# Signs and bucket pattern of an LSH attention over 128 rows, and a list schedule with other durations

## The chip, the cores and the metric

The kernel runs on one core of a Trainium2 chip. The metric is the device time of one execution in microseconds; the median of several executions is compared.

## What is computed

The reference is an attention in which a query sees only the keys of its own hash bucket, and two gated feed-forward layers after it.

```python
q_bits = (np.einsum('bhsd,dk->bhsk', q, proj) > 0)      # 6 bits; k the same
q_bucket = np.sum(q_bits * powers, axis=-1)             # a number from 0 to 63
mask = q_bucket[:, :, :, None] == k_bucket[:, :, None, :]
scores = np.where(mask, scale * q @ k.T, -1e9)          # then softmax, then @ v
x = ((x @ w1) * (x @ w2)) @ w3 @ w_out                  # 1536 tokens, 512 -> 1024 -> 512
out = (sigmoid(x @ w_gate) * (x @ w_val)) @ w_out2      # 512 -> 1536 -> 512
```

There are 2 batches of 8 heads, 768 positions and a head size of 64. The weights of the feed-forward layers come as 64-bit floats and are decoded to 32 bits on the chip.

## The kernel before, in words

**Attention.** The 16 heads are taken in order, each in 6 tiles of 128 queries; there are 96 such steps. A step multiplies scores for 128 queries and 768 keys (`emit_qk`, lines 465 and 468, two halves of 384 columns each), takes their maximum on VectorE (line 474), the exponential on ScalarE (line 484), turns the result by TensorE transposes (line 517), splits it into a rounded and a rest part (lines 520 and 522), and multiplies by the values (line 535). A float32 product is made of three matmuls of type float32r, rounded by rounded, rounded by rest, rest by rounded.

**The bucket mask.** `prep` (line 394) prepares a head while the one before it is computed. POOL scales and splits q and k (lines 404 to 406), and SyncE copies halves between partitions (lines 409 to 419). For each half of 384 positions `hashes` (line 383) makes the mask rows. Three matmuls (line 388) project q and k onto the 6 hash directions, with weights `pq` of 64 columns of which two groups of 6 are not zero; so the sums `ps[0:64]` have 64 rows. ScalarE takes their signs into `sg`, 64 rows (line 390). A fourth matmul (line 391) multiplies the signs by the pattern `pat`, 64 rows by 128 columns: row groups of signs against all 64 buckets, for q and for k. VectorE compares the sums with a threshold (line 413; for the first head line 451). The first head is prepared in `first_head` (line 424), the others in `prep`. The constants `pq`, `pat`, `zb` and the integer tiles `bits` are made once, in lines 800 to 824.

**Filler work.** Between the attention steps TensorE also multiplies w3 by w_out (line 590, `gen_fill`, with splits in lines 577 to 585) and does the first feed-forward layer for the first 512 tokens (`gen_first`, line 618, with splits of its input in lines 632 and 633). Each of the 76 weight pieces of 512 KB goes through a load (line 321) and `decode` (line 326): two ScalarE activations (337, 338), two POOL operations (339, 340) and two VectorE operations (341, 346). All other feed-forward work is in `moe` (line 710), behind the attention.

**The order.** Every step is emitted with a priority. `order_engines` (line 46) then plays a list schedule over all instructions emitted up to the end of `gen_first`: each engine takes the ready instruction with the lowest priority number, `cost` (line 75) says how long it holds the engine, `step` (line 92) how long its result takes to reach another engine, and lines 218 to 220 when a load has landed. The resulting order of each engine (TensorE, ScalarE, VectorE, POOL and SyncE's queue of DMAs) is then fixed by dependencies (line 227). The instructions of `moe` are emitted behind this and stand outside the list schedule.

Of the kernel before, what the change touches and what calls it, by code (L numbers as in the profile page):

```python
# [10 lines left out]
F32 = mybir.dt.float32  # L11
F32R = mybir.dt.float32r
U32 = mybir.dt.uint32
I32 = mybir.dt.int32
# [3 lines left out]
AF = mybir.ActivationFunctionType  # L18
# [10 lines left out]
class Tiles:  # L29
# [3 lines left out]
    rings = {}  # L33
# [12 lines left out]
def order_engines(tc):  # L46
# [8 lines left out]
    rings = Tiles.rings  # L55
    N = len(ins)

    def count(x):
        n = 1
        for _, c in list(x.ap)[1:]:  # L60
            n *= c
        return n
# [12 lines left out]
    def cost(k):  # L75
        i, e, op = ins[k], eng[k], type(ins[k]).__name__
        rd = [x for x in i.ins if hasattr(x, "ap")]
        n = max([count(i.outs[0])] + [count(x) for x in rd[:1]])
        if e == "PE":
            passes = 1 if "float32r" in str(rd[0].dtype) else 2 if n == 128 else 4  # L80
            return n / 2.4 * passes + 2.5
        if e == "Activation":
            return 971 if n == 768 else 50 + n * 0.836
        if e == "Pool":
            return 60 + n * 2.3
        if e == "DVE":
            if op in ("InstTensorTensor", "InstTensorReduce") or (op == "InstTensorScalarPtr" and len(rd) > 1 and count(rd[1]) > 8):
                return 69 + n * 1.04
            return 585 if op == "InstTensorScalarPtr" and n == 384 else 69 + n * 0.52
        return 600  # L90

    step = {("Activation", "DVE"): 145, ("Activation", "PE"): 200, ("Activation", "Pool"): 170, ("DVE", "Activation"): 132,
# [53 lines left out]
    def blocked(k):  # L146
        for t in opens.get(k, ()):
            g = rings[t][0]
            if slots[g] <= 0 or queue[g][taken[g]] != t:
                return g  # L150
            if g[0] == "mw" and pools.get("wtmp"):
                return "wtmp"
        return None
# [4 lines left out]
    dma = 0.0  # L158

    def wake(g):  # L160
        for k in waiting.pop(g, ()):
            heapq.heappush(ready[eng[k]], (ins[k].bass_priority, k))

    def post(t, what, x):
        heapq.heappush(events, (t, next(tick), what, x))
# [4 lines left out]
    while events:  # L170
        now = events[0][0]
        while events and events[0][0] <= now:
            _, _, what, x = heapq.heappop(events)
            if what == "ready":
                heapq.heappush(ready[eng[x]], (ins[x].bass_priority, x))
            elif what == "slot":
                g = rings[x][0]
                slots[g] += 1
                pools[g[0]] -= 1
                wake(g)  # L180
                if not pools[g[0]]:
                    wake(g[0])
            elif what == "end":
                for u in ends[x]:
                    left[u] -= 1
                    at[u] = max(at[u], now + step.get((eng[x], eng[u]), 60))
                    if not left[u]:
                        post(at[u], "ready", u)
                for t in held.get(x, ()):
                    todo[t] -= 1  # L190
                    if not todo[t]:
                        post(now + 200, "slot", t)
        again = True
        while again:
            again = False
            for e in ranks:
                while free[e] <= now and ready[e]:
                    _, k = heapq.heappop(ready[e])
                    g = blocked(k)
                    if g is not None:  # L200
                        waiting.setdefault(g, []).append(k)
                        continue
                    for t in opens.get(k, ()):
                        g = rings[t][0]
                        slots[g] -= 1
                        taken[g] += 1
                        if slots[g] > 0 and waiting.get(g):
                            wake(g)
                            again = True
                    order[e].append(k)  # L210
                    for u in begins[k]:
                        left[u] -= 1
                        at[u] = max(at[u], now)
                        if not left[u]:
                            post(at[u], "ready", u)
                    free[e] = done = now + cost(k)
                    if e == "SP":
                        n = count(ins[k].outs[0]) * list(ins[k].outs[0].ap)[0][1] * mybir.dt.size(ins[k].outs[0].dtype)
                        dma = max(now + 1080, dma) + n / 360
                        done = dma + 900  # L220
                    post(done, "end", k)
                    post(free[e], "free", k)
# [8 lines left out]
def lsh_attention_moe_moe2_kernel(  # L231
# [20 lines left out]
    B, H, S, D = v.shape  # L252
    P = 128
    NB = proj.shape[1]
    NT = S // P
    HS = S // 2
# [13 lines left out]
    act = nc.scalar  # L270
    dve = nc.vector
    pool = nc.gpsimd
    pe = nc.tensor
# [8 lines left out]
    cst = Tiles(ctx.enter_context(tc.tile_pool(name="cst", bufs=1, side="left")), "cst", 1)  # L282
# [3 lines left out]
    psT = Tiles(ctx.enter_context(tc.tile_pool(name="psT", bufs=4, space=bass.MemoryType.PSUM)), "psT", 4)  # L286

    idf = cst.tile([P, P], F32, name="idf")
    pq_raw = cst.tile([P, NB], F32, name="pq_raw")
    pq = [cst.tile([P, D], F32R, name=f"pq{i}") for i in range(2)]  # L290
    thr = cst.tile([P, 2], F32, name="thr")
    scl = cst.tile([P, 1], F32, name="scl")
    zb = cst.tile([D, 1], F32, name="zb")
    pat = cst.tile([D, P], F32R, name="pat")
    bits = [cst.tile([D, P], I32, name=f"bits{i}") for i in range(2)]

    xall = big.tile([P, KC, NTOK], F32, name="xall")
    xraw = [xall[:, :, i * CH:(i + 1) * CH] for i in range(NSW)]
# [4 lines left out]
    psS = Tiles(att_ctx.enter_context(tc.tile_pool(name="psS", bufs=1, space=bass.MemoryType.PSUM)), "psS", 1)  # L303
    scs = [psS.tile([P, 2, 512], F32, name=f"s{i}") for i in range(2)]
    ap_ = Tiles(att_ctx.enter_context(tc.tile_pool(name="att", bufs=2, side="right")), "att", 2)
# [77 lines left out]
    def hashes(m, half):  # L383

        hs = slice(half * HS, (half + 1) * HS)
        ps = psT.tile([P, 512], F32, tag="t", name="gps")
        for n, (w, x) in enumerate(((0, "aq"), (0, "bq"), (1, "aq"))):
            pe.matmul(ps[0:D, :HS], lhsT=pq[w], rhs=m[x][:, hs], start=n == 0, stop=n == 2)  # L388
        sg = ap_.tile([D, HS], F32R, tag="sg", name="sg")
        act.activation(out=sg, in_=ps[0:D, :HS], func=AF.Sign, scale=2.0 ** 64, bias=zb)  # L390
        pe.matmul(ps[:, :HS], lhsT=pat, rhs=sg, start=True, stop=True)  # L391
        return ps

# [30 lines left out]
    def first_head():  # L424

        alloc_mats(0)
        m = mats[0]
        t = [ap_.tile([P, S], F32, tag="qk", name=f"qk0{i}") for i in range(2)]
        for r in (slice(0, D), slice(D, P)):
            sync.dma_start(out=pq_raw[r], in_=proj)  # L430
        for half in range(2):
            hs = slice(half * HS, (half + 1) * HS)
            sync.dma_start(out=t[0][:, hs], in_=qk[0][:, hs])
        for r, o in ((slice(0, D), slice(D, P)), (slice(D, P), slice(0, D))):
            sync.dma_start(out=t[1][r], in_=qk[0][o])
        load_v(0)
        yield
        for half in range(2):
            hs = slice(half * HS, (half + 1) * HS)
            act.activation(out=m["aq"][:, hs], in_=t[0][:, hs], func=AF.Copy, scale=scl[:, 0:1])  # L440
            dve.scalar_tensor_tensor(out=m["bq"][:, hs], in0=t[0][:, hs], scalar=scl[:, 0:1], in1=f(m["aq"][:, hs]),
                                     op0=ALU.mult, op1=ALU.subtract)
        load_qk(1)
        for d in ("bk", "ak"):
            pool.tensor_copy(m[d][0:D], t[1][0:D])
        act_copy(m["bk"][D:P], f(m["bq"][D:P]))
        pss = [hashes(m, half) for half in range(2)]
        act.activation(out=m["bq"][D:P], in_=t[1][D:P], func=AF.Copy, scale=SCALE)
        for d, r in (("ak", slice(0, D)), ("aq", slice(D, P))):
            for half in range(2):  # L450
                dve.tensor_scalar(out=m[d][D:P, half * HS:(half + 1) * HS], in0=pss[half][r, :HS], scalar1=thr[r, 0:1], scalar2=thr[r, 1:2],
                                  op0=ALU.is_gt, op1=ALU.mult)
        load_qk(2)
        yield
# [345 lines left out]
    start = first_head()  # L800
    next(start)
    make_identity(nc, idf)
    o = D // 2
    pool.iota(bits[0], pattern=[[0, 2], [1, D]], base=0, channel_multiplier=0)
    for r in range(0, D, o):
        pool.iota(bits[1][r:r + o], pattern=[[0, P]], base=0, channel_multiplier=1)
# [85 lines left out]
    for _ in first:  # L892
        pass
    order_engines(tc)
    prio(0, 200000)
    att_ctx.close()
# [44 lines left out]
```

## Time and profile before

| | us |
|---|---|
| median of 3 runs | 832.86 (831.72 to 833.24) |
| the profiled execution | 831.98 |
| its span, first to last instruction | 830.2 |
| TensorE busy in the span | 801.8 |
| ScalarE, VectorE, POOL busy | 513.3, 458.0, 429.5 |
| mean granted TensorE clock | 0.992 |

PE is TensorE's matmuls, PEld its loads of weights, DVE is VectorE, ACT ScalarE, SP SyncE. A row of the trace names line, engine, operation, the tiles written and read, and shapes as partitions x elements; for a matmul, 64*128 stands for weights of 64 rows and 128 columns. Matmuls are pipelined, and their ends are modelled: the distance from the start of one to the start of the next says more than the length of a record. The profiled execution took 1.8 us more than its span, and 0.9 us less than the median of the runs.

### The profile page before, as it was taken

The numbers are of one execution on the slowest core, as the hardware profiler recorded it, in microseconds if no ns is written. First come the engines' busy times: TensorE is split into PE (matmuls) and PEld (weight loads), VectorE is DVE, ScalarE is ACT, GpSimd is POOL, SyncE is SP. The second block draws the span as 40 slices with busy tenths as digits, with TensorE's granted clock in tenths as the row PEclk, the third lists the DMA queues.
The fourth block names the chain that finished last, engine by engine and source line by source line (L and its number), as shares of the span: only waits on it lengthen the run. The fifth ranks groups of instructions, "written<-read, shape, count | busy, mean of one in ns | idle before, by whom it ended". The sixth has DMA issues, their size and how long they took to land.

```text
span 830.2 us, 11487 instructions
## 1 busy us (share of the span) xinstructions
PE 801.8 (97%) x4016; PEld 657.1 (79%) x4016; DVE 458.0 (55%) x696; ACT 513.3 (62%) x944; POOL 429.5 (52%) x457
## 2 busy tenths in 40 slices
PE   5899899999999999999999999999999999999998
PEld 3577688888787888887888888888888888888886
DVE  5536787777788878977354535564522222222222
ACT  5788778787788888876455655766534333343332
POOL 5567656665466555559355556677633333333330
PEclk9999899999999999999999999999999999999999
DMA  8744547454455644131022122344001000010001
GB/s 259 199 153 129 171 125 188 130 156 112 121 147 145 147 102 128 61 137 51 1 74 79 52 77 76 103 152 135 17 1 51 1 1 1 0 52 1 0 1 51
DMA packets 28585, 74.46 MB, mean 90 GB/s; under 512 B 6128, under 2 KB 8432, under 8 KB 28528
## 3 DMA queue, kind: packets, MB, share of 16 engines
q1 hardware_dynamic: 28528, 73.73, 29.9%
q8 instruction: 32, 0.52, 0.3%
q14 instruction: 25, 0.20, 0.1%
HBM read 52.83 MB, written 3.19 MB: 67 GB/s over the span
## 4 chain that ended last, share of the span: by engine, by line
PE 86%; DVE 8%; ACT 3%; issue 1%; POOL 1%; DMA 0%; SPq 0%; DVEq 0%; POOLq 0%; ACTq 0%
PE m L695 18%; PE pa L695 17%; PE pb L695 17%; PE av L535 8%; PE tp L517 6%; PE wacc L590 5%; PE p L695 4%; PE s L465 3%; PE s L468 3%; DVE sm L474 2%; PE y L695 2%; PE gps L388 2%; DVE pt L522 2%; DVE da L341 1%; PE gps L391 1%
## 5 line engine op out<-in xcount | busy, mean ns | idle before, releaser
L735 DVE TENSOR_TENSOR pb<-pb,a 128x512 f32<-128x512 f32 x52 | 36.3, 699 | 179.0 <-PE pb L695 175.6
L474 DVE TENSOR_REDUCE sm<-s 128x1 f32<-128x768 f32 x96 | 91.0, 949 | 32.2 <-PE s L468 25.2
L689 POOL TENSOR_TENSOR wal<-xall,wah 128x512 fp32r<-128x512 f32 x36 | 46.9, 1304 | 107.2 <-ACT wah L277 107.2
L517 PE MATMUL tp<-idf,e 128*128 128x128 f32 x576 | 99.8, 278 | 1.0 <-DVE pt L522 1.0
L695 PE MATMUL pa<-x,wah 128*128 128x512 f32 x320 | 99.2, 390 | 0.0
L695 PE MATMUL pb<-x,wbh 128*128 128x512 f32 x320 | 98.6, 389 | 0.0
L520 ACT ACTIVATE pt<-tp 128x512 fp32r<-128x512 f32 (+1 forms) x144 | 82.8, 597 | 23.7 <-PE tp L517 22.6
L484 ACT ACTIVATE e<-s,sm 128x768 f32<-128x768 f32 x96 | 86.6, 902 | 13.8 <-DVE sm L474 12.4
L339 POOL TENSOR_SCALAR dr<-st 128x512 bf16<-128x512 f32 x76 | 71.0, 943 | 46.4 <-issue 25.7
L522 DVE TENSOR_TENSOR pt<-tp,pt 128x512 fp32r<-128x512 f32 x126 | 83.4, 683 | 18.1 <-ACT pt L520 17.7
L535 PE MATMUL av<-pt,spv 128*128 128x256 f32 (+1 forms) x576 | 86.0, 299 | 1.3 <-DVE pt L522 1.2
L517 PEld LDWEIGHTS tp<-idf,e 128*128 128x128 f32 x576 | 72.4, 143 | 12.5 <-issue 2.4
L535 PEld LDWEIGHTS av<-pt,spv 128*128 128x128 f32 (+1 forms) x576 | 73.7, 184 | 10.7 <-DVE pt L522 2.8
L590 PE MATMUL wacc<-wo,t 128*128 128x512 f32 x192 | 70.6, 434 | 6.3 <-ACT wo L277 2.8
L695 PEld LDWEIGHTS pa<-x,wah 128*128 128x128 f32 x320 | 60.1, 188 | 13.2
L695 PEld LDWEIGHTS pb<-x,wbh 128*128 128x128 f32 x320 | 60.1, 188 | 12.6
L465 PE MATMUL s<-bk,bq 128*128 128x384 f32 x192 | 61.8, 375 | 6.2 <-ACT e L484 5.7
L340 POOL TENSOR_SCALAR da<-da 128x512 f32<-128x512 f32 x76 | 48.3, 640 | 36.6 <-ACT da L337 32.5
L695 PE MATMUL pa<-x,wal 128*128 128x512 f32 x160 | 62.4, 391 | 0.9 <-POOL wal L689 0.9
L695 PE MATMUL pb<-x,wbl 128*128 128x512 f32 x160 | 62.5, 390 | 0.0
L468 PE MATMUL s<-ak,aq 128*128 128x384 f32 x192 | 60.2, 369 | 0.0
L338 ACT ACTIVATE dr<-st 128x512 int16<-128x512 uint32 x76 | 59.9, 788 | 0.0
(143 smaller groups left out, 1810.2 us busy)
## 6 DMA issues: line engine op xcount, KB each, us to landing
st<-in_moe_w_dram SPq DMA_DIRECT2D x32, 512.0 KB, 4.3
st<-in_moe_w_out_dram SPq DMA_DIRECT2D x20, 512.0 KB, 4.3
st<-in_moe_w_gate_dram SPq DMA_DIRECT2D x12, 512.0 KB, 3.2
st<-in_moe_w_val_dram SPq DMA_DIRECT2D x12, 512.0 KB, 3.2
qk<-in_qk_dram SPq DMA_DIRECT2D x15, 384.0 KB, 4.2
rr<-row SPq DMA_DIRECT2D x16, 192.0 KB, 3.5
out_dram<-o SPq DMA_DIRECT2D x12, 256.0 KB, 2.0
ak<-aq SPq DMA_DIRECT2D x15, 192.0 KB, 2.6
```

The costliest lines, as they stand in the source:

```text
L338: act.activation(out=r.bitcast(I16)[:, 0::2], in_=lw, func=AF.Copy, scale=2.0 ** -29)
L339: pool.tensor_scalar(out=r.bitcast(BF16)[:, 1::2], in0=f(hw), scalar1=0.0, scalar2=1.0, op0=ALU.mult, op1=ALU.mult)
L465: pe.matmul(s[:, half, :HS], lhsT=m["bq"][:, qs], rhs=m["bk"][:, ks], start=True, stop=False)
L468: pe.matmul(s[:, half, :HS], lhsT=m["aq"][:, qs], rhs=m["ak"][:, ks], start=False, stop=True)
L474: dve.tensor_reduce(out=b, in_=s[:, :, :HS], op=ALU.max, axis=AX.XY, negate=True)
L484: act.activation(out=e.rearrange("p (a c) -> p a c", a=2), in_=s[:, :, :HS], func=AF.Exp, bias=sm, scale=1.0, accum_out=su_t[h][:, t:t + 1],)
L517: pe.transpose(ps[:, i * P:(i + 1) * P], e_t[g - g % 2 + a][:, c * P:(c + 1) * P], idf)
L520: act.activation(out=dh, in_=src, func=AF.Copy)
L522: dve.tensor_tensor(out=d, in0=src, in1=f(dh), op=ALU.subtract)
L535: pe.matmul(acc[:w.shape[1], :2 * P].rearrange("p (a t) -> p a t", a=2), lhsT=w, rhs=r[:, :, c], start=(c == 0 and i == 0), stop=(c == NT ...
L590: pe.matmul(acc, lhsT=t3[x][:, j], rhs=wo[y][:, j], start=(j == 0 and n == 0), stop=(j == NF1 - 1 and n == 2))
L695: mm = pe.matmul(ps, lhsT=lhs[x], rhs=rhs[y], start=start and n == 0, stop=stop and n == 2)
```

## The change

The hash weights `pq` become 128 columns wide (the added columns are zero), so the sums fill 128 rows; the signs `sg`, their bias `zb` and the pattern `pat` get 128 rows too, of which the added rows of the pattern are zero. The integer tiles `bits` move from constants of their own into the ring of the mask tile `ft`. In the list schedule the durations of `cost` and the landing of a load are given other numbers, with a distinction between operands in PSUM and others.

```diff
@@ cost
+        banks = [x for x in rd + [i.outs[0]] if (region(x) or ("",))[0] in rings and rings[region(x)[0]][0][0] in ("psT", "psS")]
         if e == "PE":
             passes = 1 if "float32r" in str(rd[0].dtype) else 2 if n == 128 else 4
-            return n / 2.4 * passes + 2.5
+            return n / 2.4 * passes + (16 if passes == 1 else -12 if passes == 2 else 4)
         if e == "Activation":
-            return 971 if n == 768 else 50 + n * 0.836
+            return 971 if n == 768 and banks else 50 + n * (0.836 if banks else 1.0)
         if e == "Pool":
-            return 60 + n * 2.3
+            if op == "InstTensorTensor":
+                return 40 + n * 2.4 if n < 768 else 2200
+            return 100 + n * 1.15
         if e == "DVE":
+            if op == "InstCustomDveAnt":
+                return 720
             if op in ("InstTensorTensor", "InstTensorReduce") or (op == "InstTensorScalarPtr" and len(rd) > 1 and count(rd[1]) > 8):
-                return 69 + n * 1.04
-            return 585 if op == "InstTensorScalarPtr" and n == 384 else 69 + n * 0.52
+                return 69 + n * (1.04 if banks else 1.4)
+            return 585 if op == "InstTensorScalarPtr" and n == 384 else 69 + n * 0.6
@@ order_engines
-                        dma = max(now + 1080, dma) + n / 360
+                        dma = max(now + 1900, dma) + n / 300
                         done = dma + 900
@@ constants
-    pq = [cst.tile([P, D], F32R, name=f"pq{i}") for i in range(2)]
+    pq = [cst.tile([P, P], F32R, name=f"pq{i}") for i in range(2)]
-    zb = cst.tile([D, 1], F32, name="zb")
-    pat = cst.tile([D, P], F32R, name="pat")
-    bits = [cst.tile([D, P], I32, name=f"bits{i}") for i in range(2)]
+    zb = cst.tile([P, 1], F32, name="zb")
+    pat = cst.tile([P, P], F32R, name="pat")
@@ hashes
-            pe.matmul(ps[0:D, :HS], lhsT=pq[w], rhs=m[x][:, hs], start=n == 0, stop=n == 2)
-        sg = ap_.tile([D, HS], F32R, tag="sg", name="sg")
-        act.activation(out=sg, in_=ps[0:D, :HS], func=AF.Sign, scale=2.0 ** 64, bias=zb)
+            pe.matmul(ps[:, :HS], lhsT=pq[w], rhs=m[x][:, hs], start=n == 0, stop=n == 2)
+        sg = ap_.tile([P, HS], F32R, tag="sg", name="sg")
+        act.activation(out=sg, in_=ps[:, :HS], func=AF.Sign, scale=2.0 ** 64, bias=zb)
@@ setup
     make_identity(nc, idf)
+    bits = ap_.tile([P, S], F32R, tag="ft", name="bits", bufs=1).bitcast(I32)
+    bits = [bits[0:D, i * P:(i + 1) * P] for i in range(2)]
```

## Rows read from the trace of the kernel before

**Rows 1.** The page: TensorE's busy time; the core's span and clock.

```profile
PE 801.8 (97%) x4016; PEld 657.1 (79%) x4016; DVE 458.0 (55%) x696; ACT 513.3 (62%) x944; POOL 429.5 (52%) x457
...
core 0: 830.2 us, clock 0.992
```

**Rows 2.** Busy time by stage: stage, length, engines (instructions), clock, DMA share, GB/s.

```profile
0.00:20.00 20.00, 10.07 (x28) 6.29 (x29) 11.18 (x30) 11.62 (x19) 11.22 (x22) 0.96 0.81 261
20.00:40.00 20.00, 16.75 (x82) 11.71 (x82) 12.04 (x18) 14.76 (x29) 11.06 (x15) 0.93 0.75 203
...
80.00:100.00 20.00, 16.33 (x87) 13.46 (x88) 15.92 (x23) 15.04 (x30) 12.71 (x17) 0.83 0.54 162
...
220.00:240.00 20.00, 17.95 (x111) 14.74 (x111) 19.23 (x30) 17.34 (x36) 11.30 (x14) 1.00 0.47 134
...
376.00:830.00 454.00, 450.34 (x1954) 366.65 (x1954) 174.49 (x260) 215.61 (x364) 203.08 (x180) 1.00 0.13 45
...
100.00:376.00 276.00, 268.88 (x1660) 230.50 (x1658) 224.02 (x339) 223.14 (x440) 163.35 (x194) 1.00 0.48 131
```

**Rows 3.** The list of TensorE's waits: us in total, times, longest.

```profile
PE gps L388 <- ACT aq L440: 6.7, 1, 6.7
PE s L465 <- ACT e L484: 5.7, 6, 1.4
```

**Rows 4.** The timeline of TensorE from 300.7 to 302.6 us: start, length, instruction.

```profile
300.68 0.34 PE L468 MATMUL s<-ak,aq 128*128 128x384 f32 x1
300.86 0.34 PE L388 MATMUL gps<-aq,pq 128*64 128x384 f32 x1
301.04 0.39 PE L695 MATMUL p<-xl,wh 128*128 128x512 f32 x1
301.36 0.44 PE L391 MATMUL gps<-sg,pat 64*128 64x384 f32 x1
301.73 0.50 PE L695 MATMUL p<-xh,wl 128*128 128x512 f32 x1
302.07 0.39 PE L695 MATMUL p<-xh,wh 128*128 128x512 f32 x1
302.30 0.33 PE L388 MATMUL gps<-bq,pq 128*64 128x384 f32 x1
```

**Rows 5.** Pattern matmuls, from 100 to 376 us (ns: least/median/most) and in all.

```profile
L391 PE MATMUL gps<-sg,pat x22: 435/439/442, 103.7 to 322.4; 64*128 64x384 f32 x22
...
L391 PE MATMUL gps<-sg,pat 64*128 64x384 f32 x32 | 14.6, 461 | 1.2 <-ACT sg L390 1.2
```

**Rows 6.** The timeline of TensorE: the first scores.

```profile
11.29 1.62 PE L465 MATMUL s<-bk,bq 128*128 128x384 f32 x4 [0.27 <-ACT bq L448]
```

**Rows 7.** Groups of weight loads: count, busy us, mean ns, idle before.

```profile
L465 PEld LDWEIGHTS s<-bk,bq 128*128 128x128 f32 x192 | 35.2, 194 | 15.6 <-ACT e L484 10.5 <-issue 1.6 <-ACT da L337 0.3
...
L388 PEld LDWEIGHTS gps<-aq,pq 128*64 128x64 f32 x64 | 9.0, 140 | 10.2 <-ACT aq L440 7.0 <-POOL bq L406 0.9 <-issue 0.6
```

**Rows 8.** Groups of ScalarE's instructions: count, busy us, mean ns, idle before.

```profile
L520 ACT ACTIVATE pt<-tp 128x512 fp32r<-128x512 f32 x126 | 72.5, 598 | 20.9 <-PE tp L517 19.7
...
L390 ACT ACTIVATE sg<-gps,zb 64x384 fp32r<-64x384 f32 x32 | 17.8, 572 | 6.1 <-PE gps L388 5.7
```

**Rows 9.** Groups of VectorE's instructions: the memsets of the hash weights.

```profile
L813 DVE MEMSET pq<- 128x64 f32 x2 | 0.2, 112 | 0.1
```

**Rows 10.** Groups on POOL and VectorE, and loads (us to landing), whose planned durations change.

```profile
L339 POOL TENSOR_SCALAR dr<-st 128x512 bf16<-128x512 f32 x76 | 71.0, 943 | 46.4 <-issue 25.7 <-DVE w1r L346 10.1 <-DVE wc L346 5.6
L340 POOL TENSOR_SCALAR da<-da 128x512 f32<-128x512 f32 x76 | 48.3, 640 | 36.6 <-ACT da L337 32.5
...
L633 DVE TENSOR_TENSOR xl<-xall,xh 128x512 fp32r<-128x512 f32 x4 | 4.2, 1066 | 0.0
...
st<-in_moe_w_dram SPq DMA_DIRECT2D x32, 512.0 KB, 4.3
```

**Rows 11.** The timeline of TensorE in the stretch from 80 to 100 us.

```profile
87.36 0.62 PE L465 MATMUL s<-bk,bq 128*128 128x384 f32 x2 [1.32 <-ACT e L484]
```

## The prediction

> **What bounds the kernel now.** I read the busy times first. TensorE is busy for 801.8 of 830.2 us at a mean granted clock of 0.992 [rows 1], so what it does not do, and what it does slowly, is nearly the whole question. Then the busy times by stage. From 376 us on there is no hole but the last store: 450.34 busy of 454.00, and nothing that the diff touches runs there, so I take it as fixed. Everything that can move lies ahead of 376 us. From 100 to 376 us TensorE is busy for 268.88 of 276.00 us, against 224.02 for VectorE and 223.14 for ScalarE [rows 2]: TensorE is the bound there, with some 19% of room on the next two engines. The holes are in four short stretches: 9.93 us in 0:20, 3.25 in 20:40, 3.67 in 80:100 (which also has a granted clock of 0.83) and 2.05 in 220:240, where VectorE is busy for 19.23 of 20.00 us. The list of waits says what ends them: the first hash matmul waits 6.7 us for the first rounded input, and later the scores wait 5.7 us in six pieces for a softmax activation [rows 3].
>
> A busy engine can still be slow, and the busy share does not show that. So I read the matmuls one by one around a sign pattern (line 391) by their starts, since the ends are modelled [rows 4]. Of 384 columns, a score matmul (128 rows, 128 columns of weights) starts 0.18 us before the next one, and so does a hash matmul (128 rows, 64 columns). Of 512 columns, a matmul in plain sequence takes 302.07 to 302.30, 0.23. The pattern matmul has the same 384 columns but weights of 64 rows. The matmul ahead of it takes 301.04 to 301.36, 0.32 in place of 0.23; it takes 301.36 to 301.73, 0.37 in place of 0.18; the one behind it takes 301.73 to 302.07, 0.34 in place of 0.23. Together 0.09 + 0.19 + 0.11 = 0.39 us of TensorE's time that buys nothing. The group is uniform: the 22 pattern matmuls between 100 and 376 us last 435 to 442 ns, and there are 32 in all [rows 5], one for each half of each of 16 heads.
>
> **The change, part by part.** 1. *Pattern over 128 rows.* The weights and the signs fill all rows, as in every matmul around them. I take the 0.39 us as the price of changing from 128 rows to 64 and back, since the hash matmuls, which differ from their neighbours in columns only, show nothing of it. For 22 in the bound stretch: 22 x 0.39 = 8.6 us. I count nine tenths, 7.7, since that stretch is busy to 97% (268.88 of 276.00) and a little of what is freed will meet waits. Of the other ten, two stand at the start, where the scores start at 11.29 us when ScalarE's copy of line 448 is done [rows 6]: nothing gained. Eight lie between 20 and 82 us: 8 x 0.39 = 3.1, among the holes of 20:40 and 80:100; I count half, 1.6. Sum 9.3 us. Bounds: 0, if all of it turns into waits, and 8.6 + 3.1 = 11.7.
>
> 2. *Hash weights of 128 columns.* 96 matmuls of line 388 get weights twice as wide. A load of 64 columns takes 140 ns, one of 128 columns 194 [rows 7]: 96 x 0.054 = 5.2 us if the loads were exposed, nothing if they hide behind the running matmul. I take nothing: the score matmul with its 128 columns has the same 0.18 us from start to start as the hash matmul with 64. The matmul ahead of it covers the load (0.18 us against 0.194 and overlapping); without that cover it is the 5.2.
>
> 3. *Sign activation on 128 partitions.* 32 activations of 64x384 take 572 ns; the copies of 128x512 out of the same kind of tile take 598 [rows 8], so twice the partitions cost between 0 and 32 x 0.026 = 0.8 us of ScalarE, which has room. I take nothing, as a row of 384 elements stays one of 384.
>
> 4. *Setup.* Wider memsets and the bit tiles in the ring of the mask tile run while TensorE waits its first 6.7 us [rows 3]. The next user of that ring is the second head's mask, which comes behind the first head's scores at 11.29 us [rows 6]. Nothing; without the cover, the two memsets of 112 ns [rows 9] once more, 0.2 us.
>
> 5. *The list schedule.* No work is added, but every engine's order up to the end of attention and of the first token chunk can change, with SyncE's queue of loads and POOL's among them. A load out of turn holds back all that stand behind it on SyncE; a decode out of turn holds POOL's splits, and through them the matmuls that read them. What the plan believed and what the trace has [rows 10]: POOL's two decode steps were planned at 60 + 512 x 2.3 = 1238 ns each and take 943 and 640; the new 100 + 512 x 1.15 = 689 is nearer in sum (1378 against 1583, before 2476). VectorE's split of line 633 was planned at 601, takes 1066, is now 786. A 512 KB load was planned to land after 1080 + 1456 + 900 = 3.4 us, takes 4.3, is now 4.5. For TensorE, 384 columns go from 162.5 to 176, the 0.18 of the trace. So the plan comes nearer nearly everywhere, yet a list schedule answers to a small change with another order, and another order has other holes. Bounds: at best it clears the holes after the start, 3.25 + 3.67 + 2.05, and the clock lost in 80:100, 0.17 x 20 = 3.4, together 12.4 us. At worst it digs the same again, 12.4. I take a gain of 2.0, the row it is nearest to: the hole of 220:240, where line 633 holds VectorE's queue, is the one whose cause the new durations speak of most directly.
>
> The sum: the profiled execution took 831.98 us. 831.98 - 9.3 - 2.0 = 820.7. The median of the runs shown is 832.86, 0.9 above it; so 821.5 us for the median.
>
> **The rivals.** A. *The freed time turns into waits.* TensorE gets to each wait sooner, and VectorE and ScalarE, each busy for over 80% of 100:376, come last more often; 220:240 shows how that looks. For it: scores already wait for the softmax. Against it: 97% busy with only 7.1 us of holes in 276. Half of 8.6 stays, nothing of the first 100 us and nothing of the plan: 832.86 - 4.3 = 828.6 us.
>
> B. *The plan starves TensorE (slower).* Place: the fill work of the first 100 us, where matmuls of line 590 wait for a decoded and split weight. That is how 80:100 looks now: a hole of 1.32 us [rows 11] and others, 3.67 in all, and then matmuls at the lower of the two clock levels (1.2 in place of 2.4 GHz) for part of the stretch, 3.4 us. One such stall costs 7.1 us. It decides from the second one on, as one does not use up the 9.3: 832.86 - 9.3 + 14.2 = 837.8 us. For it: POOL's plan falls by 1.1 us a decode to below what is measured, so splits may be ordered to be ready sooner than they are. Against it: the loads are planned later, not earlier.
>
> C. *The plan clears that stall.* With 7.1 us of 80:100 and the 2.0 taken: 832.86 - 9.3 - 9.1 = 814.5 us. For it: later landings in the plan are just what a stall on decoded weights asks for. Against it: some hole has always been left somewhere.
>
> D. *The pattern stays dear and the hashes get dearer.* If a load of weights went beside a running matmul only where their rows differ, 128 rows after 128 rows would save nothing at the pattern, and the wider hash loads would show: 832.86 + 5.2 = 838.1 us. Against it: the score matmuls load 194 ns of 128-row weights each [rows 7] and still start 0.18 us apart [rows 4]. The Trainium skill, page "TensorE: Matmul & The Clock Gate", section "The mechanism", states this rule: loads overlap with matmuls in flight only when the row group differs. By that rule the change would lose; the trace's start to start disagrees with it, so the case gets little.
>
> **How the numbers follow.** Forecast 0.60, A 0.20, C 0.11, B 0.06, D 0.03. Predicted: the forecast's 821.5. The range runs from C's 814 to just past A's 829; B and D, and the far sides of A and C, are left out, under 2 in 10. The unknown of the schedule, not the pattern, sets its width. A change within 0.2% (1.7 us) is about what measurement cannot tell from none. Faster by more: the forecast and C, and most of A, 0.87. Within: the rest of A, 0.04. Slower: B and D, 0.09.
>
> **What would show it.** Right: in the new trace line 391 lasts about as long as line 388 (some 340 ns), starts 0.18 us ahead of the next matmul, and its neighbours are back to 0.23 for 512 columns; line 388 still starts 0.18 apart; the end of the attention comes some 11 us sooner; and the stretch behind it keeps its length to a microsecond. Wrong: line 391 still at 0.37 (D); TensorE's holes ahead of the end of attention growing by over 4 us, on waits for VectorE or ScalarE (A), or on line 590 with a granted clock under 0.9 beside it (B). The schedule is right if the holes of 220:240 and 80:100 shrink or go and none of their size comes elsewhere.

## The result and the profile after

The changed kernel takes 814.43 us (median of 4 runs, 814.15 to 815.14), the kernel before 833.05 in the runs beside it: a ratio of 0.9778, 95% interval 0.9761 to 0.9795, so 18.5 us less. Its profiled execution took 815.14 us.

The page of the changed kernel, as [rows 1]:

```profile
PE 790.9 (97%) x4016; PEld 659.0 (81%) x4016; DVE 459.3 (56%) x696; ACT 512.7 (63%) x944; POOL 432.7 (53%) x457
...
core 0: 813.4 us, clock 0.998
```

TensorE's matmuls are as many and its busy time is 10.9 us shorter; the span is 16.8 shorter. So a part of the gain is busy time that went and a part is holes that went, and the mean clock is higher too. The busy times by stage, as [rows 2] (the end of the attention lies some 17 us sooner, so the last two stages are cut at 360):

```profile
0.00:20.00 20.00, 10.10 (x24) 6.74 (x24) 12.78 (x32) 11.06 (x19) 10.71 (x21) 1.00 0.77 265
20.00:40.00 20.00, 17.89 (x92) 13.98 (x93) 10.41 (x16) 16.20 (x32) 15.09 (x21) 0.91 0.73 202
...
80.00:100.00 20.00, 18.37 (x119) 15.91 (x119) 19.94 (x31) 18.03 (x36) 15.95 (x22) 1.00 0.82 218
...
200.00:220.00 20.00, 18.56 (x120) 16.15 (x120) 16.15 (x25) 16.30 (x34) 10.02 (x14) 1.00 0.46 126
220.00:240.00 20.00, 19.44 (x125) 17.04 (x123) 18.57 (x29) 17.94 (x36) 13.49 (x16) 1.00 0.51 142
...
100.00:360.00 260.00, 255.40 (x1609) 225.63 (x1608) 213.15 (x326) 214.92 (x425) 156.07 (x181) 1.00 0.50 131
360.00:813.00 453.00, 449.69 (x1953) 366.06 (x1951) 173.89 (x259) 215.67 (x364) 202.35 (x179) 1.00 0.13 45
```

A stage's hole is its length less TensorE's busy time. The hole of 80:100 falls from 3.67 to 1.63 us, and the granted clock there goes from 0.83 to 1.00, so no part of that stretch runs at the lower level any more. It does 119 matmuls where there were 87. That of 20:40 falls from 3.25 to 2.11, with the clock still at 0.91. The hole of 220:240 falls from 2.05 to 0.56, but most of it has only moved: the stage ahead of it, 200:220, had 0.38 in the kernel before.

```profile
200.00:220.00 20.00, 19.62 (x118) 16.18 (x117) 12.41 (x19) 13.27 (x26) 10.01 (x12) 1.00 0.37 101
```

It has 1.44 now, so the two together fall from 2.43 to 2.00. From 100 us to the end of the attention the holes fall from 7.12 us (in 276) to 4.60 (in 260). The stretch behind the attention keeps its length. The matmuls of the second layer's half (tile m), first the kernel before, then the changed one; the last two times of a row are its first and last start:

```profile
L695 PE MATMUL m<-wth,gl x144: 395/396/397, 539.3 to 826.1; 128*128 128x512 f32 x144
L695 PE MATMUL m<-gh,wth x64: 392/397/400, 417.0 to 532.5; 128*128 128x512 f32 x64
```

```profile
L699 PE MATMUL m<-wth,gl x144: 395/396/397, 522.5 to 809.3; 128*128 128x512 f32 x144
L699 PE MATMUL m<-gh,wth x64: 392/397/400, 400.1 to 515.7; 128*128 128x512 f32 x64
```

From the first to the last it is 409.1 us before and 409.2 after: all 16.9 us were won ahead of it. Now the pattern matmul (line 395 in the changed kernel), in TensorE's timeline of two stretches, as [rows 4]:

```profile
286.12 0.40 PE L699 MATMUL p<-xh,wh 128*128 128x512 f32 x1
286.36 0.34 PE L395 MATMUL gps<-sg,pat 128*128 128x384 f32 x1
286.54 0.34 PE L392 MATMUL gps<-bq,pq 128*128 128x384 f32 x1
...
287.52 0.33 PE L469 MATMUL s<-bk,bq 128*128 128x384 f32 x1
287.72 0.44 PE L395 MATMUL gps<-sg,pat 128*128 128x384 f32 x1
288.00 0.34 PE L469 MATMUL s<-bk,bq 128*128 128x384 f32 x1
288.18 0.39 PE L699 MATMUL p<-xh,wh 128*128 128x512 f32 x1
```

At 286.36 nothing is left of the 0.39 us: 0.24 ahead, 0.18 for itself, 0.17 behind. At 287.72 it takes 0.28, with 0.20 ahead and 0.18 behind. This second form is common here: between 100 and 360 us the 20 records last from 333 to 446 ns, and 11 of them 440 or more. The loads of the weights show the difference, first in the kernel before with the signs that it reads, then the two of the changed kernel:

```profile
300.47 0.58 ACT L390 ACTIVATE sg<-gps,zb 64x384 fp32r<-64x384 f32 x1 [1.66 <-PE gps L388]
...
301.36 0.18 PEld L391 LDWEIGHTS gps<-sg,pat 64*128 64x128 f32 x1 [0.30 <-ACT sg L390]
```

```profile
286.20 0.19 PEld L395 LDWEIGHTS gps<-sg,pat 128*128 128x128 f32 x1
...
287.72 0.19 PEld L395 LDWEIGHTS gps<-sg,pat 128*128 128x128 f32 x1 [0.24 <-ACT sg L394]
```

Before, the load of 64 rows starts only with its own matmul, at 301.36, though the signs, which its wait names, were done at 301.05. With 128 rows it starts at 286.20, 0.16 us ahead of its matmul, and hides behind the matmul in front. At 287.72 it again starts together with its matmul, but here because the signs are only just there: the waits of this tile name ScalarE's signs as what these loads waited for (2.3 us in 9 waits between 100 and 360 us). Such a late load shows by 0.10 us, a quarter of the old price.

### The profile page after: what moved, and what is told of

It is laid out like the page before. It is cut to its first block, busy times and chain, and to the rows that moved or that the text cites. A ratio compares the mean times of both kernels' runs of the same rounds, so it can differ in the third digit from the quotient of the medians.

```text
span 813.4 us, 11496 instructions
## 1 busy us (share of the span) xinstructions
PE 790.9 (97%) x4016; PEld 659.0 (81%) x4016; DVE 459.3 (56%) x696; ACT 512.7 (63%) x944; POOL 432.7 (53%) x457
## 4 chain that ended last, share of the span: by engine, by line
PE 85%; DVE 9%; POOL 2%; ACT 2%; issue 2%; DMA 0%; SPq 0%; ACTq 0%; DVEq 0%; POOLq 0%
PE m L699 18%; PE pa L699 18%; PE pb L699 18%; PE av L539 7%; PE tp L521 6%; PE p L699 5%; PE wacc L594 3%; PE s L469 3%; PE y L699 3%; PE s L472 3%; DVE pt L526 2%; DVE sm L478 2%; DVE da L345 2%; PE gps L392 1%; DVE w3f L350 1%
## 5 line engine op out<-in xcount | busy, mean ns | idle before, releaser
L488 ACT ACTIVATE e<-s,sm 128x768 f32<-128x768 f32 x96 | 86.7, 906 | 12.4 <-DVE sm L478 11.9
L521 PEld LDWEIGHTS tp<-idf,e 128*128 128x128 f32 x576 | 72.3, 142 | 10.9 <-DVE pt L526 1.5
L594 PE MATMUL wacc<-wo,t 128*128 128x512 f32 x192 | 68.5, 424 | 0.8 <-ACT wo L282 0.8
```

The lines of the kernel that those rows point to most:

```text
L488: act.activation(out=e.rearrange("p (a c) -> p a c", a=2), in_=s[:, :, :HS], func=AF.Exp, bias=sm, scale=1.0, accum_out=su_t[h][:, t:t + 1],)
L521: pe.transpose(ps[:, i * P:(i + 1) * P], e_t[g - g % 2 + a][:, c * P:(c + 1) * P], idf)
L594: pe.matmul(acc, lhsT=t3[x][:, j], rhs=wo[y][:, j], start=(j == 0 and n == 0), stop=(j == NF1 - 1 and n == 2))
```

## The experiments

Each kernel was timed in turn with the kernel before, on the same chip. Numbers 1, 2, 3 and 5 ran together, 6 to 9 together, and 10 to 13 together, each group beside its own runs of the kernel before; so the ratios are what to compare.

| kernel | rows of the pattern | durations in the plan | us | ratio to before, 95% |
|---|---|---|---|---|
| before | 64 | old | 832.2 to 833.1 | 1 |
| e3_wide_hash_only | 64, hash weights 128 wide | old | 833.02 | 1.0011 (1.0001 to 1.0021) |
| e1_pattern_only | 128 | old | 825.56 | 0.9914 (0.9900 to 0.9927) |
| e2_durations_only | 64 | new | 820.16 | 0.9852 (0.9837 to 0.9867) |
| the changed kernel | 128 | new | 814.43 | 0.9778 (0.9761 to 0.9795) |
| e10_old_pe_plus1 | 128 | old, TensorE 1 ns longer | 822.58 | 0.9886 (0.9871 to 0.9900) |
| e11_old_dma_plus50 | 128 | old, loads 50 ns later | 825.25 | 0.9914 (0.9900 to 0.9929) |
| e12_old_pool_plus5 | 128 | old, POOL 5 ns longer | 822.74 | 0.9887 (0.9870 to 0.9903) |
| e9_pe_plus1 | 128 | new, TensorE 1 ns longer | 817.01 | 0.9810 (0.9796 to 0.9824) |
| e6_pool_old | 128 | new, POOL old | 817.34 | 0.9817 (0.9803 to 0.9832) |
| e7_actdve_old | 128 | new, ScalarE and VectorE old | 816.26 | 0.9802 (0.9787 to 0.9816) |
| e5_pe_old | 128 | new, TensorE old | 811.20 | 0.9746 (0.9729 to 0.9763) |
| e8_dma_old | 128 | new, loads old | 810.44 | 0.9729 (0.9713 to 0.9745) |
| e13_pe_dma_old | 128 | new, TensorE and loads old | 808.00 | 0.9708 (0.9694 to 0.9723) |

**The two parts apart.** The plan's `cost` counts elements of a row, not rows, so the number of rows changes no engine's order after the setup: the pattern alone runs in the order of the kernel before, and the durations alone in the order of the changed kernel. The traces bear this out: all 4016 matmuls come in the same order in each of these pairs. That makes four kernels of two orders by two patterns. The pattern alone, against the changed kernel:

```diff
-            return n / 2.4 * passes + (16 if passes == 1 else -12 if passes == 2 else 4)
+            return n / 2.4 * passes + 2.5
...
-                        dma = max(now + 1900, dma) + n / 300
+                        dma = max(now + 1080, dma) + n / 360
```

> The old durations stay, so every engine keeps the order of the kernel before; only hash weights, signs and pattern fill 128 rows. Theory P (a change from 128 to 64 rows costs 0.39 us and back, and most of that time is kept): about 9 us faster than before, 822 to 825 us, and line 391 starts 0.18 to 0.28 us ahead of the next matmul instead of 0.37. Rival S (the new order brings most of the gain, and in the old order the freed time turns into waits): under 5 us faster, 828 us or more.

Measured: 825.56 us, 7.1 less than before (6.1 to 8.3 by the interval). The same place as [rows 4], in the timeline of TensorE of this kernel:

```profile
294.79 0.34 PE L388 MATMUL gps<-aq,pq 128*128 128x384 f32 x1
294.96 0.40 PE L695 MATMUL p<-xl,wh 128*128 128x512 f32 x1
295.20 0.34 PE L391 MATMUL gps<-sg,pat 128*128 128x384 f32 x1
295.37 0.40 PE L695 MATMUL p<-xh,wl 128*128 128x512 f32 x1
295.61 0.40 PE L695 MATMUL p<-xh,wh 128*128 128x512 f32 x1
```

The matmul ahead takes 0.24, the pattern 0.17, the one behind 0.24. In the same order, with the same neighbours, 0.32, 0.37 and 0.34 are gone. So the 0.39 us was the price of the 64 rows. The time lies 0.6 us above Theory P's 822 to 825 and well below Rival S's 828: P's mechanism holds, at 7 rather than 9 us. Of the 30 x 0.39 = 11.7 us that it counted, 7.1 were kept.

The durations alone:

```diff
-    pq = [cst.tile([P, P], F32R, name=f"pq{i}") for i in range(2)]
+    pq = [cst.tile([P, D], F32R, name=f"pq{i}") for i in range(2)]
...
-        sg = ap_.tile([P, HS], F32R, tag="sg", name="sg")
+        sg = ap_.tile([D, HS], F32R, tag="sg", name="sg")
```

> 64 rows as before, new durations, so every engine has the order of the changed kernel. Theory P: the rest of the gain, 18.6 - 9 = about 9 us, so 823 to 825 us, with line 391 at 0.37 us again. Rival S: 13 us or more faster, 820 us or less. If the two parts only work together, both runs stay above 827 us.

Measured: 820.16 us, 12.3 less than before (11.1 to 13.6). This is near Rival S's 820 and below Theory P's 823 to 825: the new order is worth more than P's 9 and a little less than S's 13. So P was nearly right on the pattern alone, and S on the order alone. The two parts add up: 0.9914 x 0.9852 = 0.9767, and the changed kernel stands at 0.9778, inside its interval. In the new order the pattern is worth 0.9778 / 0.9852 = 0.9925, some 6 us.

Where the order's 12 us come from, in the busy times by stage: first the kernel before, then the durations alone.

```profile
0.00:100.00 100.00, 82.54 (x405) 59.90 (x406) 59.44 (x99) 74.53 (x142) 63.05 (x85) 0.93 0.61 181
100.00:400.00 300.00, 292.69 (x1764) 250.14 (x1763) 238.54 (x354) 235.74 (x462) 182.81 (x208) 1.00 0.45 124
```

```profile
0.00:100.00 100.00, 86.84 (x452) 64.19 (x453) 71.27 (x112) 81.27 (x155) 74.43 (x98) 1.00 0.71 202
100.00:400.00 300.00, 296.85 (x1769) 253.27 (x1769) 232.12 (x344) 232.38 (x454) 178.74 (x197) 1.00 0.46 117
```

TensorE's holes shrink by 4.3 us in the first 100 us (17.46 to 13.16) and by 4.2 behind (7.31 to 3.15), and the mean granted clock of the first 100 us goes from 0.93 to 1.00. Between the profiled executions, 831.98 and 820.17, lie 11.8 us; 8.5 of them are holes. The 3.3 that remain are TensorE's busy time, which falls from 801.8 to 798.2 us for the same 4016 matmuls. That fits the clock, which by an estimate from the mean of 0.93 was 0.07 x 100 = 7 us short, partly in holes; how much of the 3.3 it is was not measured. POOL is busy for 74.43 of the first 100 us, before for 63.05: the decodes come earlier, 16 of them by then where there were 12.

**The wide hash weights.** Against the pattern alone, this kernel puts the signs and the pattern back to 64 rows and keeps the rest, the new place of the bit tiles too:

```diff
-    pat = cst.tile([P, P], F32R, name="pat")
+    pat = cst.tile([D, P], F32R, name="pat")
...
-        sg = ap_.tile([P, HS], F32R, tag="sg", name="sg")
-        act.activation(out=sg, in_=ps[:, :HS], func=AF.Sign, scale=2.0 ** 64, bias=zb)
+        sg = ap_.tile([D, HS], F32R, tag="sg", name="sg")
+        act.activation(out=sg, in_=ps[0:D, :HS], func=AF.Sign, scale=2.0 ** 64, bias=zb)
```

> Old order; hash weights of 128 columns, but signs and pattern of 64 rows as before. Theory P (loads of 128 columns hide behind the running matmul): no difference, within 1 us of before, line 388 still 0.18 us from start to start. Rival D (the loads show): 5 us slower than before.

Measured: 833.02 us beside 832.61. By the interval the difference is 0.1 to 1.7 us: at most a little, and far from the 5 us of Rival D. Its loads of hash weights, and a pattern in its timeline:

```profile
L388 PEld LDWEIGHTS gps<-aq,pq x64: 186/188/338, 6.7 to 320.9; 128*128 128x128 f32 x64
```

```profile
301.17 0.34 PE L388 MATMUL gps<-aq,pq 128*128 128x384 f32 x1
301.35 0.40 PE L695 MATMUL p<-xl,wh 128*128 128x512 f32 x1
301.68 0.44 PE L391 MATMUL gps<-sg,pat 64*128 64x384 f32 x1
302.05 0.51 PE L695 MATMUL p<-xh,wl 128*128 128x512 f32 x1
```

A load takes 188 ns where it took 140 [rows 7], and the matmul still starts 0.18 us ahead of the next: hidden. The pattern, left at 64 rows, keeps its price: 0.33 ahead and 0.37 for itself. Rival D falls. And since this kernel differs from the pattern alone by the rows of signs and pattern only, the 7.5 us between them (833.02 and 825.56) belong to these rows.

**Which durations.** One group at a time was put back to its old numbers, in the changed kernel.

```diff
-            return n / 2.4 * passes + (16 if passes == 1 else -12 if passes == 2 else 4)
+            return n / 2.4 * passes + 2.5
```

> The changed kernel with TensorE's old planned durations (2.5 ns over the columns), all others new. If the gain of the plan comes from TensorE's durations, most of its 9 us go: 822 to 824 us. If it comes from the other engines and the loads, 814 to 817 us. If any change of the plan throws the dice anew, anywhere between 812 and 824 us without pattern.

Measured: 811.20 us, 3 us faster than the changed kernel. TensorE's longer durations, which agree with the trace, brought no gain in this order.

```diff
-            if op == "InstTensorTensor":
-                return 40 + n * 2.4 if n < 768 else 2200
-            return 100 + n * 1.15
+            return 60 + n * 2.3
```

> The changed kernel with POOL's old planned durations (a decode at 2476 ns instead of 1378), all others new. Theory C (the plan gains because a few large errors of the old durations go): POOL's was the largest in a decode, so 4 us or more of the plan's 12 us come back, 818 us or more. Rival R (any other order falls somewhere in the same scatter, whichever duration is changed): 811 to 818 us, like the run with TensorE's old durations at 811.

Measured: 817.34 us, 3 us slower: short of Theory C's 818, and inside Rival R's range.

```diff
-            return 971 if n == 768 and banks else 50 + n * (0.836 if banks else 1.0)
+            return 971 if n == 768 else 50 + n * 0.836
...
-                return 69 + n * (1.04 if banks else 1.4)
+                return 69 + n * 1.04
```

> The changed kernel with ScalarE's and VectorE's old planned durations, all others new. Theory C: these are planned 60 to 200 ns too short again for each operand out of SBUF, on engines that are busy to 80%, so 2 to 6 us come back, 816 to 820 us. Rival R: 811 to 818 us.

Measured: 816.26 us, 2 us slower, inside the ranges of both theories, so it decides nothing.

```diff
-                        dma = max(now + 1900, dma) + n / 300
+                        dma = max(now + 1080, dma) + n / 360
```

> The changed kernel with the old landing of loads (3.4 us for 512 KB instead of 4.5, measured 4.3 before), all others new. Theory C: decodes and filler matmuls are planned too soon again in the first 100 us, the stalls of 20:40 and 80:100 come back with their lower clock, 5 us or more: 819 us or more. Rival R: 811 to 818 us.

Measured: 810.44 us, 4 us faster. Theory C of this run fails clearly: the stall does not come back. Its stretch from 80 to 100 us, by stage:

```profile
80.00:100.00 20.00, 19.26 (x124) 16.90 (x123) 19.85 (x31) 17.45 (x35) 14.83 (x19) 1.00 0.79 223
```

A nonsense step shows how much of this is chance:

```diff
-            return n / 2.4 * passes + (16 if passes == 1 else -12 if passes == 2 else 4)
+            return n / 2.4 * passes + (17 if passes == 1 else -12 if passes == 2 else 4)
```

> The changed kernel with each float32r matmul planned 1 ns longer (17 in place of 16): no better and no worse a likeness of the trace. What it differs by measures the scatter of the list schedule itself. Theory C: within 1.5 us of the changed kernel, 813 to 816 us. Rival R: several us away, on either side.

Measured: 817.01 us. One nanosecond in the plan of a matmul moves the time by 2.6 us, as much as POOL's or ScalarE's and VectorE's whole groups put back. That is above Theory C's 813 to 816. By these five runs alone, R could hold: all orders lie between 810 and 817.

**Good plan or good luck.** So the old plan was given the same kind of nonsense steps, with 128 rows. The three edits are shown against the pattern alone.

```diff
-            return n / 2.4 * passes + 2.5
+            return n / 2.4 * passes + 3.5
```

> Old durations with 128 rows (825.6 us), but each float32r matmul planned 1 ns longer (3.5 in place of 2.5): the same small step that moved the new plan by 2.6 us. Theory C (the new durations make a better plan, with scatter of some 3 us on top): 820 to 829 us, above all five orders of the new kind (810 to 817). Rival R (the old order was one bad draw of the same scatter): 811 to 819 us.

```diff
-                        dma = max(now + 1080, dma) + n / 360
+                        dma = max(now + 1130, dma) + n / 360
```

> Old durations with 128 rows, each load planned to land 50 ns later (1130 in place of 1080), which says nothing new of the chip. Theory C: 820 to 829 us. Rival R: 811 to 819 us.

```diff
-            return 60 + n * 2.3
+            return 65 + n * 2.3
```

> Old durations with 128 rows, each POOL operation planned 5 ns longer (65 in place of 60), which says nothing new of the chip. Theory C: 820 to 829 us. Rival R: 811 to 819 us.

Measured: 822.58, 825.25 and 822.74 us, with 825.56 for the old plan itself. Four orders of the old kind lie between 822.6 and 825.6; seven of the new kind (the next run among them) between 808.0 and 817.3. The ranges do not touch; between them lie 5.2 us. The holes of TensorE in the first 100 us part in the same way: 16.9 to 18.4 us in the four, 11.9 to 14.9 in the seven. So the old order was no bad draw, and a real gain of the new durations stands above a scatter of some 3 us. Five of the seven have one or two groups of durations put back, and only two are the new plan whole or moved by a nanosecond; the seven show what the new numbers are worth in groups, not how one plan scatters.

```diff
-            return n / 2.4 * passes + (16 if passes == 1 else -12 if passes == 2 else 4)
+            return n / 2.4 * passes + 2.5
...
-                        dma = max(now + 1900, dma) + n / 300
+                        dma = max(now + 1080, dma) + n / 360
```

> 128 rows, new durations for POOL, ScalarE and VectorE, old ones for TensorE and the loads: both were better old when tried alone (811.2 and 810.4 us). If each carried a gain of its own, 803 to 809 us. If they were draws of the scatter, anywhere from 808 to 817 us. In both cases far below 825.6, if POOL, ScalarE and VectorE carry what is real in the new plan.

Measured: 808.00 us, the fastest kernel here, 6 us below the changed one. POOL's, ScalarE's and VectorE's new durations carry the whole gain of the plan without the others. Which of these engines it takes is not shown: each of the two groups put back cost 2 to 3 us, no more than the scatter, and neither was tried alone in the old plan. Whether the old figures for TensorE and the loads are better in themselves stays open: 6 us is twice the scatter, but it is one order.

**What the plan had wrong.** The list of waits of POOL, cut at 100 us, has one line that tells the plans apart: the split of w_out (`wo`), whose second step stands in POOL's queue and needs ScalarE's rounding. The numbers are us in total, times, longest. The kernel before:

```profile
POOL wo L585 <- ACT wo L277: 16.1, 6, 4.1
```

The old plan with loads 50 ns later:

```profile
POOL wo L585 <- ACT wo L278: 16.3, 6, 3.7
```

The durations alone:

```profile
POOL wo L589 <- ACT wo L282: 2.6, 3, 1.9
```

The changed kernel with POOL's old durations:

```profile
POOL wo L587 <- ACT wo L280: 14.9, 6, 5.8
```

With ScalarE's and VectorE's old durations:

```profile
POOL wo L587 <- ACT wo L280: 4.4, 4, 2.7
```

The fastest kernel:

```profile
POOL wo L589 <- ACT wo L282: 1.9, 2, 1.5
```

With each of POOL's two decode steps planned at 1238 ns, POOL stands still for 13 to 16 us of the first 100 behind a split that is not ready, and the decodes queued behind it stand too; with POOL's new durations, for 1 to 4. So it is in all the kernels here, with POOL's group put back alone too (14.9). But the wait is not shown to be what the gain hangs on: with POOL old and all else new, it is back, yet the kernel is only 3 us slower than the changed one and 5 faster than the best order of the old plan. What ScalarE's and VectorE's durations did in its place was not traced to a wait.

## Why the prediction was right, and where it was off

**Direction and bound.** TensorE was the bound up to the end of the attention, the stretch behind it did not change, and both edits made it faster. 814.43 lies inside the range, 0.4 us from its fast end of 814; the forecast of 821.5 was 7 us too slow. That it fell inside is partly luck: one nanosecond in the plan moved the time by 2.6 us, and three of the orders tried (811.20, 810.44 and 808.00) lie outside. The two sizes that were off also pulled in opposite directions, the pattern 2 to 3 us too high and the order 10 too low. Of what it named as signs, the stretch behind the attention kept its length as said, and the end of the attention came 17 us sooner, not 11.

**Step 1, the pattern.** The mechanism was right and so was its price: the 0.39 us goes where the order is held and only the rows change. The share kept was put too high: 9.3 us taken, 7.1 measured in the old order and some 6 in the new. "A little of what is freed will meet waits" was more than a little: of the 11.7 us counted, six tenths were kept, where the step took nine tenths in the bound stretch and half ahead of it. Of the 4.6 us lost in the old order, 1.3 are found as holes (82.54 to 82.05 busy in the first 100 us, 292.69 to 291.88 in the next 300). Another 2.7 never came free: TensorE's busy time falls by 9.0 us, from 801.8 to 792.8, not by 11.7. A part of that is the late load, as six of the 22 pattern matmuls between 100 and 376 us still last over 400 ns; the rest could not be placed by rows. The sign that line 391 would last some 340 ns and start 0.18 us ahead of the next matmul came true for 8 of the changed kernel's 20 pattern matmuls between 100 and 360 us; 11 others last 440 ns or more, and start 0.28 ahead. Rival A was a part of the truth.

**Steps 2 to 4.** Nearly nothing, as taken: 0.4 us between the medians for the wide hash weights and the new place of the bit tiles, with the load covered as step 2 said. The sign activation takes 582 ns on 128 partitions where it took 576 (medians), 0.2 us over all 32. The Trainium skill, page "TensorE: Matmul & The Clock Gate", section "The mechanism", has loads overlap with matmuls in flight only where the row group differs; here loads of 128 rows hide behind matmuls of 128 rows (188 ns, with 0.18 us from start to start), and the loads that show are those of 64 rows, and a few of 128 whose input comes late. The runs decide against that sentence, for this kernel.

**Step 5, the list schedule.** This is the term that was mis-sized: a gain of 2.0 us taken, 12.3 measured, just at its best bound of 12.4. The step took the hole of 220:240 as nearest, and in the changed kernel that hole mostly moved to the stage ahead of it (the pair falls from 2.43 to 2.00 us), against the sign that none of it comes elsewhere. The better row to be near was the first 100 us: behind the first 20 us, whose hole of 9.9 stays, they had 7.5 us of holes, of which 4.3 went, and the clock was low there alone. The other 4.2 us of holes went between 100 us and the end of the attention. The largest error that the step itself listed, 2476 against 1583 ns for POOL's part of a decode, acts in the first 100 us, where the decodes and splits of w_out feed line 590.

**Rival C** named the outcome, 814.5 us with the stall of 80:100 cleared: its clock is full again and its hole 1.63 us. But its reason was wrong, and its number met the measured one by chance. It gave later landings in the plan as the cause, and with the old landings that stage's clock is full too, its hole is 0.74, and the kernel is 4 us faster. **Rival B** took POOL's shorter plan for a danger; no run shows one, and with POOL's old plan back the kernel is 3 us slower. **Rival D** fell by its own run.

## What to carry to other kernels

A matmul whose weights fill 64 rows among neighbours of 128 was paid for in half by the neighbours: compare starts, not lengths, and fill the rows with zeros if nothing else uses them. When a schedule is planned from durations, look in the trace for an engine that stands still behind something that is not ready (here POOL), and expect each new set of numbers to throw the order anew: try a few neighbours of the plan, judge a change of the durations by the group of them, and keep the fastest. The plan closer to the trace in nearly every number was not the fastest one.

## What was not expected of the hardware

One matmul with weights of 64 rows among matmuls of 128 costs 0.39 us more, over twice its own 0.18, and its load of weights does not start before its matmul does. Changing the columns of the weights (64 to 128 and back, line 388) costs nothing that the starts show. The only two matmuls of 64 rows that follow each other, at the start, wait for their signs, so whether the price is that of the change or of the 64 rows themselves stays open. And with 128 rows a matmul whose input comes just in time still shows 0.10 us of its load of weights, with a record of 440 ns in place of 333: in the trace the idle time of the load, too, is ended by the signs.
